# Windowed attention and soft routing on one core: values loaded straight into block-diagonal places, memory keys spread on chip, the dispatch maximum kept per token tile

## The chip, the cores and the metric

The kernel runs on one core of a Trainium2 chip. The metric is the device time of one execution in microseconds (us). The core's engines work side by side, each on its own list of instructions in order: PE (matrix products, with PEld its weight loads), DVE (vector), ACT (scalar functions), POOL (general) and SP, which here only issues DMA transfers. An engine waits at an instruction until what it needs is there; all instructions behind it wait too. SBUF is the on-chip memory of 128 partitions; PSUM takes the results of PE in eight banks.

## The reference

Three stages follow each other; 3072 tokens, 512 features.

```python
# 1. attention: 4 batches, 8 heads, head size 64, in chunks of 32 tokens
for c in range(nc):
    ...                          # keys: 16 to the left, 32 own, 8 to the right
    k_full = np.concatenate([mem_k, k_ctx], axis=2)     # and 8 memory keys in front
    v_full = np.concatenate([mem_v, v_ctx], axis=2)
    scores = scale * np.matmul(q_c, k_full.transpose(0, 1, 3, 2))
    scores = scores - np.max(scores, axis=-1, keepdims=True)
    a = np.exp(scores)
    a = a / (np.sum(a, axis=-1, keepdims=True) + 1e-09)
    out[:, :, c_start:c_end] = np.matmul(a, v_full)
# 2. soft mixture of 8 experts with 4 slots each (32 slots)
logits = x @ phi
d = softmax(logits, over tokens); slot_input = d.T @ x       # dispatch
for e in range(E):
    h = np.maximum(slot_input[e] @ w1[e], 0.0)
    slot_out[e] = h @ w2[e]
x = softmax(logits, over slots) @ slot_out                   # combine
# 3. last layer, 512 -> 1024 -> 512
h = x @ w_in
solu = h * softmax(h)
ln = (solu - mean) / np.sqrt(var + 1e-06) * g_ln
return ln @ w_out
```

## The kernel before

Attention runs in 32 groups. A group is two heads (a pair) of half the sequence of one batch: 384 tokens, 12 chunks. The two heads lie on partitions 0 to 63 and 64 to 127 of `kq`, which holds keys and queries transposed. Four groups (the four pairs of a half batch, `hb`) give three token tiles of 128 tokens with all 512 features in `xb`, and there are eight half batches.

The loop over `g` (lines 796 to 824) is software-pipelined, and its order is written by hand (`manual_schedule`): an iteration issues the QK matmuls of group g+1 (`emit_qk`), the softmax of g+1 (`emit_softmax`, whose second half normalizes the result of g-2), the loads, the PV matmuls of g-1 (`emit_pv`), the steps of the dispatch that fall due (`todo`), transposes of the outputs of g-3 (`emit_xt`) and of the exponentials of g (`emit_t`), the exp of g+1, the copy of values for g+1 (`emit_vspread`), the spread of keys for g+3 (`emit_spread`), and pieces of the conversion of w_in (`casts`).

A window of a chunk has 64 keys. The keys come in 13 records of 40 columns, 32 tokens and the 8 memory keys again in every record; `emit_spread` copies the two heads' halves into `kz`, which is block-diagonal: each head's keys have zeros on the other head's partitions, so that one matmul yields both heads. Which engine copies which half is in `SPR` ("a" ACT, "d" DVE, "p" POOL). The values likewise come as 128 rows (64 window places of each head) into `vb` and are copied by POOL into the block-diagonal `vz` (`emit_vspread`, `move`, line 294).

All large loads are issued on SP: `load_qk` (line 185, four buffers `kq`), `load_v` (line 194, four buffers `vb`), and `load_e`, which takes the next weight chunk of 512 KB from the list `chunks` (80 of them: w_in and w_out first, then the 64 of the experts in the order of use) into the next free slot; without a slot it issues none. `LOADS[g]` says how many chunks an iteration may issue. After the loop it issues as many as there are slots; later slots come free as the expert units use theirs (`release`), and the code lets SP wait for that.

The dispatch is a softmax over tokens with a running maximum: per half batch, `emit_lg` computes the logits in four partial sums on four partition blocks, ACT copies them (line 328), a matmul with `i4rep` (line 331) adds them up on every block, DVE takes the maximum over 384 tokens (line 334), ACT the exp (line 339) and a copy of the logits (line 344), three transposes and two copies (`emit_turn`, line 354) bring both to token rows, and `emit_dacc` adds to `acc`, scaled by `alpha`. Line 376 keeps the sum of the exponentials. After the last half batch `emit_slots` makes the slot inputs; then come 32 expert units (`emit_w1`, `emit_w2`), the combine softmax beside them, and the last layer, 24 token tiles.

## Time and profile before

| what | value |
|---|---|
| time, median of 3 runs | 337.04 us (336.84 to 337.57) |
| the profiled execution's own time | 337.29 us |
| its span, first to last instruction | 335.5 us |
| PE, PEld busy | 305.7 us (91%), 214.7 us (64%) |
| DVE, ACT, POOL busy | 247.1 (74%), 240.1 (72%), 192.6 us (57%) |
| HBM read, written | 80.11 MB, 16.78 MB |
| chain that ended last, by engine | PE 60%, DMA 16%, DVE 9%, ACT 8%, POOL 3% |

Busy shares are averages over stages with different limits, so they do not say what bounds the time. For that one reads the stretches of the span by themselves, which transfers are under way in them, and in the chain what each stretch waited for last. The chain is followed back from the last instruction, at each step to what released it.

### The profile page before, as it was taken

Reading aid. Unit: us, or ns where it says so; the run is one execution under the profiler, and the core shown is the slowest. Engines: PE = TensorE matmul, PEld = TensorE weight load, DVE = VectorE, ACT = ScalarE, POOL = GpSimd, SP = SyncE. Lnnn points to the kernel's source line nnn. Section 1 sums busy time; section 2 is a strip of 40 time slices with the busy share of each in tenths; the row PEclk is TensorE's granted clock in tenths of the full one; section 3 lists DMA queues with packets and bytes.
Section 4 is the critical chain, followed back from the end, with each engine's and each line's share of the span. In section 5 each row is a group of like instructions: output and inputs, shape, how many; then the busy total and the mean of one; then the engine's idle time right before and its main releaser. Section 6 shows DMA issues by size and latency. Waiting matters only on the chain.

```text
span 335.5 us, 8126 instructions
## 1 busy us (share of the span) xinstructions
PE 305.7 (91%) x2964; PEld 214.7 (64%) x2964; DVE 247.1 (74%) x445; ACT 240.1 (72%) x453; POOL 192.6 (57%) x381
## 2 busy tenths in 40 slices
PE   1998798898997989878999899999999999999995
PEld 1675565666665543322334688888888888888885
DVE  4796987988899337999207885896887989688540
ACT  3587868869886527675524879897897999788631
POOL 5587989797899113223100357776767577476600
PEclk9999999999999999999999999999999999999999
DMA  7999999999999999999950004747675675767531
GB/s 266 414 412 414 412 411 414 413 409 412 402 408 411 413 419 419 406 416 417 419 238 0 0 34 156 250 161 257 213 259 212 217 252 172 266 220 249 191 95 64
DMA packets 38920, 97.42 MB, mean 290 GB/s; under 512 B 4320, under 2 KB 14944, under 8 KB 38880
## 3 DMA queue, kind: packets, MB, share of 16 engines
q1 hardware_dynamic: 38736, 96.68, 75.2%
q8 instruction: 23, 0.38, 0.5%
q10 hardware_dynamic: 144, 0.22, 0.4%
q14 instruction: 17, 0.14, 0.1%
HBM read 80.11 MB, written 16.78 MB: 289 GB/s over the span
## 4 chain that ended last, share of the span: by engine, by line
PE 60%; DMA 16%; DVE 9%; ACT 8%; POOL 3%; issue 2%; SPq 0%; ACTq 0%; DVEq 0%; POOLq 0%
PE bank L687 36%; DMA ex_area<-in_w_dram 6%; DMA e_area<-in_w_dram 6%; DMA kq_area<-in_kr_dram 4%; PE bank L306 4%; PE h L599 4%; POOL v_area L294 2%; PE bank L246 2%; PE bank L368 2%; PE bank L317 2%; PE bank L325 1%; PE bank L461 1%; ACT s_area L278 1%; ACT s_area L320 1%; ACT kq_area L290 1%
## 5 line engine op out<-in xcount | busy, mean ns | idle before, releaser
L687 PE MATMUL bank<-wh_area,yh_area 128*128 128x512 f32 x552 | 129.6, 390 | 0.0
L687 PEld LDWEIGHTS bank<-wh_area,yh_area 128*128 128x128 f32 x552 | 103.4, 188 | 21.8
L294 POOL TENSOR_SCALAR v_area<-v_area 64x780 f32<-64x780 f32 x64 | 57.6, 900 | 14.7 <-DMA v_area<-in_vr_dram 4.8
L670 DVE STREAM_TRANSPOSE yq_area<-yq_area 128x1024 f32<-128x1024 f32 x20 | 24.9, 1245 | 23.2 <-DMA yq_area<-z 23.2
L246 PE MATMUL bank<-kq_area 128*32 128x128 f32 x768 | 29.5, 290 | 9.4 <-ACT kq_area L290 7.4
L306 PE MATMUL bank<-v_area,s_area 128*32 128x130 f32 x768 | 28.4, 280 | 8.4 <-ACT s_area L286 4.0
L677 ACT CAST yh_area<-yq_area 128x1024 fp32r<-128x1024 f32 x20 | 21.0, 1049 | 16.1 <-DVE yq_area L670 16.1
L653 POOL TENSOR_SCALAR cst_area<-cst_area 128x1 f32<-128x1 f32 x72 | 28.1, 390 | 7.1
L614 DVE SCALAR_TENSOR_TENSOR eb_area<-h,eb_area 128x1024 f32<-128x1024 f32 x24 | 28.8, 1202 | 4.6 <-ACT eb_area L608 4.3
L652 POOL TENSOR_SCALAR cst_area<-cst_area 128x1 f32<-128x1 f32 x72 | 25.8, 359 | 7.7
L246 PEld LDWEIGHTS bank<-kq_area 128*32 128x32 f32 x768 | 20.3, 114 | 15.5 <-ACT kq_area L290 9.7
L605 DVE TENSOR_REDUCE cst_area<-h 128x1 f32<-128x1024 f32 x24 | 29.0, 1216 | 0.9 <-PE h L599 0.9
L306 PEld LDWEIGHTS bank<-v_area,s_area 128*32 128x32 f32 x768 | 20.3, 110 | 14.2 <-ACT s_area L286 4.8
L608 ACT ACTIVATE eb_area<-h,cst_area 128x1024 f32<-128x1024 f32 x24 | 26.6, 1108 | 1.9 <-DVE cst_area L605 1.9
L290 ACT COPY kq_area<-kq_area 64x512 f32<-64x512 f32 x39 | 23.7, 609 | 5.8 <-DMA kq_area<-in_kr_dram 5.6
L637 ACT ACTIVATE eb_area<-eb_area,cst_area 128x1024 f32<-128x1024 f32 x24 | 27.3, 1139 | 0.1
L681 DVE TENSOR_TENSOR yh_area<-yq_area,yh_area 128x1024 fp32r<-128x1024 f32 x20 | 24.6, 1228 | 2.3 <-ACT yh_area L677 2.3
L634 ACT ACTIVATE eb_area<-eb_area,cst_area 128x1024 f32<-128x1024 f32 x20 | 23.1, 1154 | 2.4 <-DVE eb_area L614 1.4
L264 DVE TENSOR_REDUCE cst_area<-bank 128x6 f32<-128x384 f32 x32 | 17.7, 552 | 7.1 <-PE bank L246 6.6
L641 POOL TENSOR_SCALAR cst_area<-cst_area 128x1 f32<-128x1 f32 x24 | 9.0, 375 | 21.9 <-ACT eb_area L608 20.0
L320 ACT COPY s_area<-bank 128x384 f32<-128x384 f32 x32 | 15.4, 481 | 8.2 <-PE bank L317 8.0
L643 POOL TENSOR_SCALAR cst_area<-cst_area 128x1 f32<-128x1 f32 x24 | 6.4, 267 | 23.4 <-ACT eb_area L637 22.8
(150 smaller groups left out, 573.8 us busy)
## 6 DMA issues: line engine op xcount, KB each, us to landing
e_area<-in_w_dram SPq DMA_DIRECT2D x37, 512.0 KB, 8.8
kq_area<-in_kr_dram SPq DMA_DIRECT2D x32, 448.0 KB, 7.0
ex_area<-in_w_dram SPq DMA_DIRECT2D x26, 512.0 KB, 9.9
v_area<-in_vr_dram SPq DMA_DIRECT2D x32, 390.0 KB, 7.2
z<-eb_area SPq DMA_DIRECT2D x20, 512.0 KB, 3.1
yq_area<-z SPq DMA_DIRECT2D x80, 128.0 KB, 2.8
out_dram<-eb_area SPq DMA_DIRECT2D x23, 256.0 KB, 2.6
e_area<-in_w_in_dram SPq DMA_DIRECT2D x8, 512.0 KB, 8.1
```

The source lines that it names most:

```text
L246: pe.matmul(out=bk[32 * j:32 * j + 32, t * 128:(t + 1) * 128], lhsT=kq[i][:, KS + c * CH:KS + (c + 1) * CH], rhs=kwin(g % 2, c), start=Tru ...
L290: act.copy(out=o, in_=i)
L294: pool.tensor_scalar(out=o, in0=i, scalar1=1.0, scalar2=0.0, op0=ALU.mult, op1=ALU.add)
L306: pe.matmul(out=bk[32 * j:32 * j + 32, t * 2 * VW:(t + 1) * 2 * VW], lhsT=atb[g % 2][:, c * CH:(c + 1) * CH], rhs=vz[g % 2][:, :, c * VW:( ...
L605: dve.tensor_reduce(out=sc("nm", i), in_=fin["h"][i % 2], axis=AX.X, op=ALU.max, negate=True)
L608: act.activation(out=eb[i % FIN], in_=fin["h"][i % 2], func=ACTF.Exp, bias=sc("nm", i), accum_out=sc("s", i))
L614: dve.scalar_tensor_tensor(out=ub[i % FIN], in0=fin["h"][i % 2], scalar=-1.0 / FF, in1=eb[i % FIN], op0=ALU.mult, op1=ALU.mult, accum_out= ...
L637: act.activation(out=sq, in_=ub[i % FIN], func=ACTF.Square, scale=-float(FF), bias=sc("nu", i), accum_out=sc("vs", i))
L652: pool.tensor_scalar(out=t, in0=r, scalar1=r, scalar2=xx, op0=ALU.mult, op1=ALU.mult)
L653: pool.tensor_scalar(out=r, in0=t, scalar1=1.5, scalar2=r, op0=ALU.add, op1=ALU.mult)
L670: dve.transpose(out=yv[i % FIN].rearrange("p (f a t) -> p a f t", f=FC, a=4), in_=yq[i % FIN].rearrange("p (a f t) -> p a f t", f=FC, a=4),)
L687: pe.matmul(out=fin["o"][i % 2], lhsT=a[i % FIN][:, f * 128:(f + 1) * 128], rhs=w[f], start=start, stop=stop)
```

## The change

The host now lays out each half's keys as 13 x 32 tokens with the 8 memory keys in the last columns, once; `emit_spread` makes two copies per half: the tokens, into records of 40 with gaps, and the memory keys, broadcast into the gaps. The values of the two heads are loaded by two DMAs each onto the even and the odd partitions of one of four `vz`, which are zeroed once at the start; `emit_vspread` is gone. For the two heads' places to alternate, the softmax writes its differences with a stride of two. `load_v` now stands behind `emit_pv(g - 1)`, whose buffer it fills.

In the dispatch, the logits are accumulated over features in PSUM, the three token tiles on three blocks of 32 partitions; maximum, exp and sum are taken per tile and slot (96 rows), and the running maximum is kept per tile. After the last half batch the three maxima and sums are merged (`merge_max`, `merge_scale`, `merge_sum`, `merge_end`). The copies of ACT are issued at other places in an iteration (`then`, `last`). One more weight slot is there (`NE`), and `LOADS` changes.

```diff
...
-NE = 24
+NR = GT * NSLOT
+NE = 25
...
-LOADS = [0] + [1, 1, 1, 0] * 3 + [1] * 20
+LOADS = [0] + [1, 1, 1, 0] + [1] * 28
...
-SPR = ("ap", "aa", "ap", "ad")
-DUP = ("pp",)
+SPR = ("pp", "ap")
...
-KS = GREC * REC - NMEM
+KS = GREC * REC
+KT = GREC * CH
...
-    nq = KS + GTOK
+    nq = KT + GTOK
...
-    area("a1", [("v", 4 * VS), ("vz", 4 * VS)])
...
+    area("a1", [("vz", 8 * VS)])
...
-    vb = [at("v", VS * i, VS) for i in range(4)]
-    vz = [at("vz", 2 * VS * i, 2 * VS).rearrange("p (h c) -> p h c", h=2) for i in range(2)]
+    vz = [at("vz", 2 * VS * i, 2 * VS).rearrange("p (h c) -> p h c", h=2) for i in range(4)]
...
             rows = slice(64 * h, 64 * h + 64)
-            move(on, kz[g % 2][rows, KS * h:KS * h + KS], kq[g % 4][rows, 0:KS])
+            z = kz[g % 2][rows, KS * h:KS * h + KS].rearrange("p (c r) -> p c r", r=REC)
+            own = kq[g % 4][rows, 0:GREC * CH].rearrange("p (c r) -> p c r", r=CH)
+            mem = kq[g % 4][rows, KT - NMEM:KT].rearrange("p (o r) -> p o r", o=1)
+            move(on, z[:, :, 0:CH], own)
+            move(on, z[:, :, CH:REC], mem.to_broadcast([64, GREC, NMEM]))
 
     def load_v(g):
-        sp.dma_start(out=vb[g % 4], in_=vr[g])
+        for h in range(2):
+            sp.dma_start(out=vz[g % 4][h:P:2, h, :], in_=vr[g, h])
...
+            s = sb_[g % 2].rearrange("p (t k h) -> p t h k", t=GT, h=2)
...
-            mb = mx.rearrange("p (a o) -> p a o", o=1)
-            dve.tensor_tensor(out=s, in0=bk, in1=mb.to_broadcast([P, 6, WIN]), op=ALU.subtract)
+            dve.tensor_tensor(out=s, in0=bk, in1=mx.to_broadcast([P, GT, 2, WIN]), op=ALU.subtract)
...
-    def emit_vspread(g):
-        for h in range(2):
-            rows = slice(64 * h, 64 * h + 64)
-            move(DUP[g % len(DUP)][h], vz[g % 2][rows, h, :], vb[g % 4][rows, :])
...
-                    rhs=vz[g % 2][:, :, c * VW:(c + 1) * VW],
+                    rhs=vz[g % 4][:, :, c * VW:(c + 1) * VW],
...
-        act.copy(out=xtb[:, pr, :], in_=bk[:, 0:GTOK])
-
-
-    def emit_lg(hb, b=6):
+        if copy:
+            emit_xtcopy(g, b)
+
+    def emit_xtcopy(g, b=3):
+        act.copy(out=xtb[:, g % PAIRS, :], in_=bank(b)[:, 0:GTOK])
+
+    def emit_lg(hb, b=6, copy=True):
         for k in range(KC):
-            pe.matmul(
-                out=bank(b)[32 * k:32 * k + 32, 0:GTOK], lhsT=phi[:, k, :], rhs=xtb[:, k, :], start=True, stop=True
-            )
-        act.copy(out=ptb, in_=bank(b)[:, 0:GTOK])
-
-    def emit_dmax(hb, b=7):
-        pe.matmul(out=bank(b)[:, 0:GTOK], lhsT=i4rep, rhs=ptb, start=True, stop=True)
+            for t in range(GT):
+                pe.matmul(
+                    out=bank(b)[32 * t:32 * t + 32, 0:P], lhsT=phi[:, k, :], rhs=xtb[:, k, t * P:(t + 1) * P],
+                    start=(k == 0), stop=(k == KC - 1),
+                )
+        if copy:
+            emit_lgcopy(hb, b)
+
+    def emit_lgcopy(hb, b=6):
+        act.copy(out=ptb[0:NR], in_=bank(b)[0:NR, 0:P])
+
+    def emit_dmax(hb, b=6):
+        dve.tensor_reduce(
+            out=(mcol if hb else nms[0])[0:NR], in_=bank(b)[0:NR, 0:P], axis=AX.X, op=ALU.max, negate=True
+        )
         if hb:
-            dve.tensor_copy(out=alphas[hb % 2], in_=nm)
-        dve.tensor_reduce(out=mcol if hb else nm, in_=bank(b)[:, 0:GTOK], axis=AX.X, op=ALU.max, negate=True)
+            dve.tensor_tensor(out=nms[hb % 2][0:NR], in0=mcol[0:NR], in1=nms[(hb - 1) % 2][0:NR], op=ALU.min)
+
+    def emit_dexp(hb, b=6, scale=True):
+        act.activation(
+            out=dtb[0:NR], in_=bank(b)[0:NR, 0:P], func=ACTF.Exp, bias=nms[hb % 2][0:NR],
+            accum_out=(snews[hb % 2] if hb else ssum)[0:NR],
+        )
+        if scale:
+            emit_scale(hb)
+
+    def emit_scale(hb):
         if hb:
-            dve.tensor_tensor(out=nm, in0=mcol, in1=nm, op=ALU.min)
-
-    def emit_dexp(hb, b=7):
-        act.activation(out=dtb, in_=bank(b)[:, 0:GTOK], func=ACTF.Exp, bias=nm, accum_out=snews[hb % 2] if hb else ssum)
-        if hb:
-            act.activation(out=alphas[hb % 2], in_=alphas[hb % 2], func=ACTF.Exp, scale=-1.0, bias=nm)
-
-    def emit_lcopy(hb, b=7):
-        act.copy(out=dtb[0:32], in_=bank(b)[0:32, 0:GTOK])
-
-    def emit_turn(hb, rows, dst, b=6):
-        n = len(dst) * 32
-        for j in range(GT):
-            pe.transpose(
-                out=bank(b)[:, j * n:(j + 1) * n], in_=dtb[rows:rows + n, j * 128:(j + 1) * 128],
-                identity=ident[rows:rows + n, rows:rows + n],
-            )
+            act.activation(
+                out=alphas[hb % 2][0:NR], in_=nms[(hb - 1) % 2][0:NR], func=ACTF.Exp, scale=-1.0,
+                bias=nms[hb % 2][0:NR],
+            )
+
+    def emit_turned_pe(srcs, b=6):
+        for i, src in enumerate(srcs):
+            pe.transpose(out=bank(b)[:, i * NR:(i + 1) * NR], in_=src[0:NR], identity=ident[0:NR, 0:NR])
+
+    def emit_turned_act(dst, b=6):
         for i, d in enumerate(dst):
-            act.copy(
-                out=d, in_=bank(b)[:, 0:GT * n].rearrange("p (t s) -> p t s", t=GT)[:, :, 32 * i:32 * i + 32]
-            )
+            act.copy(out=d, in_=bank(b)[:, i * NR:(i + 1) * NR].rearrange("p (t s) -> p t s", t=GT))
 
     def l_of(hb):
         return L[:, hb * GT:hb * GT + GT, :]
-
-    def emit_dt(hb):
-        emit_turn(hb, 0, [l_of(hb), Db])
...
-            dve.scalar_tensor_tensor(out=ssum, in0=ssum, scalar=alpha, in1=snews[hb % 2], op0=ALU.mult, op1=ALU.add)
+            (pool if hb < HB - 1 else dve).tensor_scalar(
+                out=ssum[0:n], in0=ssum[0:n], scalar1=alpha[0:n], scalar2=snews[hb % 2][0:n],
+                op0=ALU.mult, op1=ALU.add,
+            )
             if hb == HB - 1:
-                dve.tensor_scalar(out=rcp, in0=ssum, scalar1=1e-9, scalar2=None, op0=ALU.add)
-                dve.reciprocal(out=rcp, in_=rcp)
-                dve.tensor_scalar(out=i4s, in0=i4, scalar1=rcp, scalar2=None, op0=ALU.mult)
+                merge_sum()
             dve.scalar_tensor_tensor(
                 out=acc[0:n], in0=acc[0:n], scalar=alpha[0:n], in1=bank(b)[0:n], op0=ALU.mult, op1=ALU.add
             )
...
+    def merge_max(b=6):
+
+        nm = nms[(HB - 1) % 2]
+        dve.tensor_scalar(out=nsel[0:NR], in0=sel[0:NR], scalar1=nm[0:NR], scalar2=None, op0=ALU.mult)
+        pe.matmul(out=bank(b)[0:NR, 256:256 + GT], lhsT=i4rep[0:NR, 0:NR], rhs=nsel[0:NR], start=True, stop=True)
+        dve.tensor_reduce(out=mcol[0:NR], in_=bank(b)[0:NR, 256:256 + GT], axis=AX.X, op=ALU.min)
+
+    def merge_scale():
+        act.activation(
+            out=beta[0:NR], in_=nms[(HB - 1) % 2][0:NR], func=ACTF.Exp, scale=-1.0, bias=mcol[0:NR]
+        )
+
+    def merge_sum(b=6):
+        dve.tensor_tensor(out=rcp[0:NR], in0=ssum[0:NR], in1=beta[0:NR], op=ALU.mult)
+        pe.matmul(out=bank(b)[0:NR, 320:321], lhsT=i4rep[0:NR, 0:NR], rhs=rcp[0:NR], start=True, stop=True)
+
+    def merge_end(b=6):
+        dve.tensor_scalar(out=rcp[0:NR], in0=bank(b)[0:NR, 320:321], scalar1=1e-9, scalar2=None, op0=ALU.add)
+        dve.reciprocal(out=rcp[0:NR], in_=rcp[0:NR])
+        dve.tensor_scalar(
+            out=i4s[0:NR], in0=i4[0:NR], scalar1=beta[0:NR], scalar2=rcp[0:NR], op0=ALU.mult, op1=ALU.mult
+        )
...
-                out=bank(1)[:, k * 32:(k + 1) * 32], lhsT=acc[:, k * 128:(k + 1) * 128], rhs=i4s, start=True, stop=True
+                out=bank(1)[:, k * 32:(k + 1) * 32], lhsT=acc[0:NR, k * 128:(k + 1) * 128], rhs=i4s[0:NR], start=True, stop=True
...
+        for i in range(4):
+            for h in range(2):
+                (pool if i < 3 else dve).memset(vz[i][:, h, :], 0.0)
+            if i < 2:
+                dve.memset(kz[i][0:64, KS:2 * KS], 0.0)
+                dve.memset(kz[i][64:128, 0:KS], 0.0)
         load_qk(0)
         act.dma_start(out=at("cst", 0, NCONST), in_=cst)
+        load_qk(1)
+        load_qk(2)
         load_v(0)
-        load_qk(1)
+        load_qk(3)
         load_v(1)
-        load_qk(2)
...
         emit_spread(0, "ad")
         emit_qk(0)
         emit_spread(1, "ad")
         emit_softmax(0)
         emit_exp(0)
-        emit_vspread(0)
         emit_spread(2, "ad")
-        todo = {}
+        todo, then, last = {}, {}, {}
         for hb in range(HB - 1):
-            for k, f in ((7, emit_lg), (8, emit_dmax), (9, emit_dexp), (9, emit_lcopy), (10, emit_dt), (11, emit_dacc)):
+            for k, f in (
+                (7, lambda hb: emit_lg(hb, copy=False)), (8, emit_dmax),
+                (10, lambda hb: emit_turned_pe([dtb, ptb])), (11, emit_dacc),
+            ):
                 todo.setdefault(4 * hb + k, []).append((f, hb))
+            for k, f in (
+                (7, emit_lgcopy), (9, lambda hb: emit_dexp(hb, scale=False)), 
+                (10, lambda hb: emit_turned_act([Db, l_of(hb)])),
+            ):
+                then.setdefault(4 * hb + k, []).append((f, hb))
+            last.setdefault(4 * hb + 9, []).append((emit_scale, hb))
         casts = {}
         early = {}
         for j in range(NEARLY):
             for i in range(5):
                 casts.setdefault(int(CAST0 + CASTN * j) + i, []).append((j, i))
...
-            if g + VLEAD < GROUPS:
-                load_v(g + VLEAD)
             load_e(LOADS[g])
             if 1 <= g:
                 emit_pv(g - 1)
+            if g + VLEAD < GROUPS:
+                load_v(g + VLEAD)
             for f, hb in todo.get(g, []):
                 f(hb)
+            emit_t(g)
             if 3 <= g:
-                emit_xt(g - 3)
-            emit_t(g)
+                emit_xt(g - 3, copy=False)
             emit_at(g)
+            for f, hb in then.get(g, []):
+                f(hb)
             if g + 1 < GROUPS:
                 emit_exp(g + 1)
-                emit_vspread(g + 1)
+            if 3 <= g:
+                emit_xtcopy(g - 3)
+            for f, hb in last.get(g, []):
+                f(hb)
...
-        emit_dmax(HB - 1, 0)
+        emit_dmax(HB - 1, 3)
+        merge_max()
         emit_dacc(HB - 2, steps=(1,))
         warm(TKEEP[0])
-        emit_dexp(HB - 1, 0)
-        emit_turn(HB - 1, 32, [Db], 2)
+        emit_dexp(HB - 1, 3)
+        merge_scale()
+        emit_turned_pe([dtb], 2)
+        emit_turned_act([Db], 2)
         emit_dacc(HB - 1, 5)
+        merge_end()
         warm(TKEEP[1])
         emit_slots()
-        emit_lcopy(HB - 1, 0)
-        emit_turn(HB - 1, 0, [l_of(HB - 1)], 2)
+        emit_turned_pe([ptb], 2)
+        emit_turned_act([l_of(HB - 1)], 2)
...
-    kp = kp.reshape(B, H, NREC, CH, D)
-    kp = np.concatenate([kp, np.broadcast_to(mk[:, :, None], (B, H, NREC, NMEM, D))], 3)
-    kp = np.stack([kp[:, :, i:i + GREC].reshape(B, H, GREC * REC, D)[:, :, 0:KS] for i in (0, GCH)], 1)
-    kp = kp.reshape(B, 2, PAIRS, 2, KS, D).transpose(0, 1, 2, 3, 5, 4)
-    a["kr"] = np.concatenate([kp, qv], -1).reshape(GROUPS, P, KS + GTOK)
+    kp = np.stack([np.concatenate([kp[:, :, CH * i:CH * (i + GREC) - NMEM], mk], 2) for i in (0, GCH)], 1)
+    kp = kp.reshape(B, 2, PAIRS, 2, KT, D).transpose(0, 1, 2, 3, 5, 4)
+    a["kr"] = np.concatenate([kp, qv], -1).reshape(GROUPS, P, KT + GTOK)
...
-    a["vr"] = np.ascontiguousarray(vp).reshape(GROUPS, P, VS)
+    a["vr"] = np.ascontiguousarray(vp).reshape(GROUPS, 2, WIN, VS)
...
```

## Rows read from the trace of the kernel before

**Rows 1.** The page's second part, 40 equal slices: DMA share in tenths, GB/s.

```profile
...
DMA  7999999999999999999950004747675675767531
GB/s 266 414 412 414 412 411 414 413 409 412 402 408 411 413 419 419 406 416 417 419 238 0 0 34 156 250 161 257 213 259 212 217 252 172 266 220 249 191 95 64
...
```

**Rows 2.** Stretches: length, busy us (count) of PE, PEld, DVE, ACT, POOL; clock, DMA share, GB/s.

```profile
...
80.00:97.00 17.00, 16.51 (x327) 11.77 (x330) 14.90 (x38) 15.33 (x38) 14.01 (x16) 1.00 1.02 403
...
150.00:170.00 20.00, 18.35 (x148) 7.03 (x146) 11.57 (x28) 11.43 (x28) 4.29 (x5) 1.00 1.03 417
...
172.00:174.00 2.00, 1.61 (x8) 0.32 (x8) 0.00 (x0) 0.00 (x0) 0.00 (x0) 1.00 0.36 145
...
```

**Rows 3.** DMA packets by size; issues by line with count, size, median us to landing.

```profile
...
DMA packets 38920, 97.42 MB, mean 290 GB/s; under 512 B 4320, under 2 KB 14944, under 8 KB 38880
...
e_area<-in_w_dram SPq DMA_DIRECT2D x37, 512.0 KB, 8.8
kq_area<-in_kr_dram SPq DMA_DIRECT2D x32, 448.0 KB, 7.0
ex_area<-in_w_dram SPq DMA_DIRECT2D x26, 512.0 KB, 9.9
v_area<-in_vr_dram SPq DMA_DIRECT2D x32, 390.0 KB, 7.2
...
e_area<-in_w_in_dram SPq DMA_DIRECT2D x8, 512.0 KB, 8.1
...
```

**Rows 4.** The chain that ended last, in order of time: start us, us, what.

```profile
...
117.45 0.93 PE bank L331 x2
...
124.17 1.92 PE bank L461 x16
...
133.12 9.43 DMA e_area<-in_w_dram
...
173.59 1.05 PE bank L479 x4
...
```

**Rows 5.** The SP queue's waits: total us, times, longest.

```profile
...
SPq L185 <- PE bank L246: 34.8, 25, 3.4
...
```

**Rows 6.** DMA of a stretch of the last stage, 255 to 261 us, in 40 slices; its issues.

```profile
...
GB/s 0 0 0 41 75 239 280 287 280 246 300 280 239 273 307 260 355 348 335 362 437 410 437 382 410 369 341 355 423 301 246 123 0 0 0 0 0 0 61 55
...
yq_area<-z SPq DMA_DIRECT2D x6, 128.0 KB, 2.8
...
```

**Rows 7.** Groups by line and form, first 200 us: count, busy us, mean ns; idle before.

```profile
...
L294 POOL TENSOR_SCALAR v_area<-v_area 64x780 f32<-64x780 f32 x64 | 57.6, 900 | 14.7 <-DMA v_area<-in_vr_dram 4.8 <-issue 3.7 <-PE bank L306 2.9
...
L290 ACT COPY kq_area<-kq_area 64x512 f32<-64x512 f32 x39 | 23.7, 609 | 5.8 <-DMA kq_area<-in_kr_dram 5.6
...
L269 DVE TENSOR_TENSOR s_area<-bank,cst_area 128x384 f32<-128x384 f32 x32 | 17.8, 555 | 0.7 <-ACT kq_area L290 0.4
...
L294 POOL TENSOR_SCALAR kq_area<-kq_area 64x512 f32<-64x512 f32 x15 | 9.9, 659 | 2.6 <-DVE s_area L269 1.5
...
L292 DVE COPY kq_area<-kq_area 64x512 f32<-64x512 f32 x10 | 6.2, 620 | 4.7 <-DMA kq_area<-in_kr_dram 4.5
...
L334 DVE TENSOR_REDUCE cst_area<-bank 128x1 f32<-128x384 f32 x8 | 4.4, 550 | 3.8 <-PE bank L331 3.8
...
L328 ACT COPY s_area<-bank 128x384 f32<-128x384 f32 x8 | 3.8, 476 | 9.2 <-PE bank L368 8.6 <-PE bank L325 0.6
L344 ACT COPY s_area<-bank 32x384 f32<-32x384 f32 x8 | 3.6, 456 | 0.0
...
L376 DVE SCALAR_TENSOR_TENSOR cst_area<-cst_area 128x1 f32<-128x1 f32 x7 | 2.9, 415 | 0.2 <-ACT cst_area L341 0.2
...
L354 ACT COPY cst_area<-bank 128x96 f32<-128x96 f32 x8 | 1.9, 239 | 4.4 <-PE bank L349 4.3
...
```

**Rows 8.** The SP queue in order of time, 90 to 190 us: start us, us, issues.

```profile
...
107.78 12.46 SPq L223 DMA_DIRECT2D ex_area<-in_w_dram  x13
125.26 11.29 SPq L223 DMA_DIRECT2D e_area<-in_w_dram  x13
...
```

More of the change, by code (lines that the diff above doesn't have):

```diff
@@ L154, in tile_kernel @@
     xtb = at("xt", 0, KC * GTOK).rearrange("p (k t) -> p k t", k=KC)
-    ptb = at("pt", 0, GTOK)
-    dtb = at("dt", 0, GTOK)
+    ptb = at("pt", 0, P)
+    dtb = at("dt", 0, P)
     TB = 6
@@ L171, in tile_kernel @@
     rcp = at("misc", 288, 1)
-    nm = at("misc", 290, 1)
+    nms = [at("misc", 289 + i, 1) for i in range(2)]
     mcol = at("misc", 291, 1)
@@ L175, in tile_kernel @@
     ssum = at("misc", 293, 1)
+    beta = at("misc", 297, 1)
+    sel = at("misc", 300, GT)
+    nsel = at("misc", 304, GT)
     snews = [at("misc", 294, 1), at("misc", 296, 1)]
-    cm = at("misc", 452, NTILE // 2)
-    cs = at("misc", 464, NTILE // 2)
-    small = at("misc", 480, 192)
+    cm = at("misc", 324, NTILE // 2)
+    cs = at("misc", 336, NTILE // 2)
+    small = at("misc", 352, 192)
     FIN = 2
@@ L260, in emit_softmax @@
         if g < GROUPS:
-            bk = bank(g % 2)[:, 0:GT * 128].rearrange("p (a k) -> p a k", k=WIN)
-            s = sb_[g % 2].rearrange("p (a k) -> p a k", k=WIN)
-            mx = small[:, 0:6]
-            dve.tensor_reduce(out=mx, in_=bk, axis=AX.X, op=ALU.max)
+            bk = bank(g % 2)[:, 0:GT * 128].rearrange("p (t h k) -> p t h k", t=GT, h=2)
+            s = sb_[g % 2].rearrange("p (t k h) -> p t h k", t=GT, h=2)
+            mx = small[:, 0:6].rearrange("p (t h o) -> p t h o", t=GT, o=1)
+            dve.tensor_reduce(
+                out=small[:, 0:6], in_=bk.rearrange("p t h k -> p (t h) k"), axis=AX.X, op=ALU.max
+            )
         if n >= 0:
@@ L308, in emit_pv, with emit_xt @@
                     lhsT=atb[g % 2][:, c * CH:(c + 1) * CH],
-                    rhs=vz[g % 2][:, :, c * VW:(c + 1) * VW],
+                    rhs=vz[g % 4][:, :, c * VW:(c + 1) * VW],
                     start=True, stop=True,
                 )
-    def emit_xt(g, b=3):
+    def emit_xt(g, b=3, copy=True):
         hb, pr = divmod(g, PAIRS)
@@ new lines, in emit_dmax @@
+    def emit_dmax(hb, b=6):
+        dve.tensor_reduce(
+            out=(mcol if hb else nms[0])[0:NR], in_=bank(b)[0:NR, 0:P], axis=AX.X, op=ALU.max, negate=True
+        )
+        if hb:
+            dve.tensor_tensor(out=nms[hb % 2][0:NR], in0=mcol[0:NR], in1=nms[(hb - 1) % 2][0:NR], op=ALU.min)
[6 more added lines that the diff above has]
+            emit_scale(hb)
@@ L405, in emit_c0t @@
         pe.transpose(out=bank(5)[:, 0:128], in_=at("c0", 0, P), identity=ident)
-        act.copy(out=at("misc", 300, P), in_=bank(5)[:, 0:128])
+        act.copy(out=at("c0", 0, P), in_=bank(5)[:, 0:128])
     def combine(b):
@@ L599, in emit_h @@
             pe.matmul(
-                out=fin["h"][i % 2][:, sl], lhsT=c4t(i) if i else at("misc", 300, P), rhs=m4[:, sl] if i else mps[:, sl],
+                out=fin["h"][i % 2][:, sl], lhsT=c4t(i) if i else at("c0", 0, P), rhs=m4[:, sl] if i else mps[:, sl],
                 start=True, stop=True,
@@ L762, in tile_kernel @@
     with tc.manual_schedule():
+        for i in range(4):
[4 more added lines that the diff above has]
+                dve.memset(kz[i][64:128, 0:KS], 0.0)
         load_qk(0)
         act.dma_start(out=at("cst", 0, NCONST), in_=cst)
+        load_qk(1)
+        load_qk(2)
         load_v(0)
-        load_qk(1)
+        load_qk(3)
         load_v(1)
-        load_qk(2)
         load_v(2)
-        load_qk(3)
-        for z in kz:
-            dve.memset(z[0:64, KS:2 * KS], 0.0)
-            dve.memset(z[64:128, 0:KS], 0.0)
-        for z in vz:
-            for h in range(2):
-                pool.memset(z[64 * h:64 * h + 64, 1 - h, :], 0.0)
-        dve.memset(acc, 0.0)
-        dve.memset(ssum, 0.0)
         emit_spread(0, "ad")
@@ L794, in tile_kernel @@
                 casts.setdefault(int(CAST0 + CASTN * j) + i, []).append((j, i))
+        dve.tensor_reduce(
+            out=sel, in_=ident.rearrange("p (t s) -> p t s", t=4)[:, 0:GT, :], axis=AX.X, op=ALU.add
+        )
         for g in range(GROUPS):
@@ L836, in tile_kernel @@
             emit_xt(GROUPS - 1, 1)
-        emit_dt(HB - 2)
+        emit_turned_pe([dtb, ptb])
+        emit_turned_act([Db, l_of(HB - 2)])
         if not TORD[0]:
```

10 lines of the change are left out of this document (4 added, 6 removed).

## The prediction

> **What bounds the kernel now.** I read the slices of the page first. The DMA row is at its top digit and the rate stands at 402 to 419 GB/s in every slice from the second to the twentieth, then falls: the twenty-first, which begins at 167.75 us, moves 2.0 MB, 4.8 us at the rate before it, so the stream ends at about 172.6 us [rows 1]. Stretches say the same more finely: 403 GB/s at 80 to 97 us, 417 at 150 to 170, 145 in the last two microseconds, each with PE's clock granted in full [rows 2]. Until 172.6 us the 16 DMA engines have no gap, and what they carry is a fixed list: 32 key and query loads of 448 KB, 32 value loads of 390 KB [rows 3], and the code's list of 80 weight chunks of 512 KB: 69.6 MB in all, with one small table. Read next where the chain of waits touches this list: from 133.12 us it is one weight DMA after another until 173.59, where the last expert matmuls start [rows 4]. After that no load is waited for: the 162 us left are compute that the change does not touch. The end is therefore the end of the stream plus a constant.
>
> Between 31 and 133 us the chain runs through PE, DVE, ACT and POOL, though DMA is full there too: in 80 to 97 us, of 17.0 us, PE is busy 16.5, ACT 15.3, DVE 14.9, POOL 14.0 [rows 2]. Two things are balanced there, and each could starve the other. A group with one weight chunk carries 448 + 390 + 512 KB = 1.382 MB, 3.35 us at 413 GB/s. The SP queue runs ahead of compute only as far as the four key buffers let it: its largest wait in this stage is line 185 on PE's QK matmuls, 34.8 us in 25 pieces [rows 5]. DMAs land about 7 us after their issue [rows 3]: that backlog is the cover that keeps DMA full.
>
> **The change part by part.**
> *Fewer bytes.* A row of kr shrinks from 896 to 800 columns, 384 bytes, on 32 x 128 = 4096 rows: 1.573 MB of 69.6. By bytes alone at 413 GB/s, a middling slice, that is 3.81 us. Rows also have a fixed part. With 4 KB rows alone DMA moves 417 GB/s [rows 2], so one of sixteen engines spends 157 ns on a row; the fetches of 1 KB rows in the last stage hold 239 to 307 GB/s until the next store joins them, 272 on average [rows 6], 60.2 ns. A line through both gives 0.0316 ns per byte and 28 ns fixed; 384 bytes are 12.1 ns, times 256 rows for each engine: 3.10 us. The bounds are 3.10 and 3.81; I take 3.4, since the mix with shorter rows loses only 1% against 4 KB rows (slices of 412 and 417 [rows 1]), less than a fixed 28 ns would make it lose. [...]
>
> *Value loads in two halves.* Each 390 KB load becomes two of 195 KB on 64 alternate partitions. Rows keep their 3120 bytes and their number. Every DMA brings 16 packets under 512 bytes (4320 [rows 3], for 270 DMAs by the whole view), so 32 more DMAs are 512 more, which I take as 32 per engine; between nothing and one row's fixed part each, 0 to 0.9 us; I take 0.2. The 32 more issues occupy SP about 0.35 us each, 11 us in all, hidden in its waits of 34.8 us. The rate of a 64-row load is not in the trace. The nearest rows are the fetches on 32 partitions: 272 GB/s, of whose deficit the 1 KB rows explain an unknown part [rows 6]. The cost lies between nothing (the same rows in twice as many loads) and 12.78 MB at 272 instead of 413 GB/s, 47.0 for 30.9 us, 16.1 us. I take nothing, since rows, bytes and the 16 engines stay the same and other loads are in flight beside a half load, and keep the other end for a rival. [...]
>
> *The V copy goes.* 64 copies of 900 ns on POOL [rows 7], 1.8 us per group, disappear, and the PV matmuls read what DMA wrote. In exchange load_v(g+3) waits on PE's PV of group g-1 (before, on POOL's copy, two steps earlier), and behind it on SP wait the next key load and weight chunk. PV follows QK on PE directly, so SP is released about 0.9 us later in a group than now; that comes out of the 7 us of backlog. Value data are needed four steps after the issue, so PE does not wait for them.
>
> *Memory keys on chip.* A spread of half a group was one copy of 64x512 (ACT 609 ns, POOL 659, DVE 620 [rows 7]); it becomes one of 416 columns and one of 104. The first I scale to 0.51 on ACT and 0.55 us on POOL; the second is near the 128x96 copies of 239 ns [rows 7]. ACT does 0.5 halves per group instead of 1.25: 0.76 falls to 0.38 us. DVE's 0.25 go: 0.16. POOL does 1.5 instead of 0.5 but has lost 1.8 us: 2.13 falls to 1.2.
>
> *Dispatch per token tile.* Per half batch PE loses the 128x384 matmuls of line 331 (0.93 us in the chain [rows 4]; 0.23 per group); the twelve 128-column ones instead of four of 384 are as many columns. ACT loses line 344 (456 ns) and half of line 328's 476; DVE loses over half of line 334's 550 and line 376 (415) to POOL [rows 7]: about 0.17 and 0.18 us per group. With the spreads, DVE is 0.34 and ACT 0.55 us per group lighter. Line 269 now writes with a stride of two: between nothing and its 555 ns again [rows 7]; I take nothing, because its input in PSUM is read as before; at the other end DVE is 0.2 us per group heavier than now, which feeds the second rival. Otherwise compute can follow DMA, whose group is now 400 + 390 + 512 KB, 3.23 us.
>
> *Two more chunks early, one more slot.* The new LOADS issues 30 instead of 28 chunks in the loop, so bytes that must pass during attention fall only from 42.4 to 41.8 MB: DMA is not idled by the smaller loads. The order of the 80 chunks is the same.
>
> *The merge at the end* adds nine small instructions, each at most like line 376's 415 ns [rows 7], 3.7 us, beside the last exp, transposes and dacc. The path up to 124.17 us loses the copy and matmul of lines 328 and 331 (0.48 + 0.93) and half a reduce [rows 4, 7]; I set the two against each other. Costed at nothing, since DMA sets the end; what it costs without that cover is the second rival.
>
> Sum: -3.4 + 0.2 = -3.2 us. The profiled execution took 337.29 us, its span 335.5; it becomes 334.1. The median of three runs is 337.04, 0.25 lower: **333.8 us**.
>
> **The rivals.**
> *The half loads are slower (slower than before).* For each per cent that the value stream loses, the end moves 0.31 us. The point that decides is 10%: at 370 GB/s the gain is gone. At 23% it is 30.9/0.77 - 30.9 = 9.2 us lost, 6.0 net: 343. For it: the 32-partition fetches stay near 272 GB/s [rows 6]. Against: those have 1 KB rows and nothing else in flight. Chance 0.14.
>
> *DMA runs dry at the hand-over (smaller gain).* SP issues its last free slot at 120.24 us and goes on at 125.26, after the first expert matmuls [rows 8]; DMAs landing 9.9 us after issue cover the gap, with data until about 128. After the change the slots in front of the experts hold one more chunk but 1.57 MB less has gone before: they are full 1.05 MB, 2.5 us, earlier. If the first unit stays at 124.17, DMA is idle for 1 to 2 us. It should come 1.1 us earlier, because the last keys land that much earlier (38.4 instead of 38.9 MB are issued up to them), and earlier still by the lighter engines; if these are not lighter, or SP's later release empties the backlog, 1 to 2.5 us of 3.2 are lost: 335.5. Chance 0.13.
>
> *Nothing gained:* both of these in small measure, 337. Chance 0.06.
>
> *More gain:* the dips to 402 and 408 GB/s in the eleventh and twelfth slices [rows 1] go with the lighter engines and rows cost by bytes alone: 332.6. Chance 0.13.
>
> **How the numbers follow.** Forecast 333.1 to 334.6: 0.54. A measurement can tell 0.2%, 0.7 us, from no change. Faster takes the forecast, the larger gain and the hand-over rival: 0.80; same 0.06; slower 0.14. The range leaves out the slower rival and the last of the larger gain: 332.4 to 336.9.
>
> **What would show it.** The stream should fall to nothing at about 169 us instead of 172.6, with 410 GB/s or more in each earlier slice; the first weight matmul should start before 124; from the last expert matmuls to the end should be 162 us as now. A rate below 405 in the attention stretches with SP not waiting means the half loads are slow; a gap in the DMA row near 120 to 127 means the hand-over. The prediction is wrong if the tail changes, or if the stream's end does not set it.

## The result, and the profile after

The change takes 334.43 us, the median of four runs (332.55 to 334.67), against 337.29 us of the kernel before (336.84 to 337.57) in the same session: ratio 0.9900, 95% interval 0.9884 to 0.9915, 2.9 us faster. The profiled execution took 334.36 us, its span 332.5. In a second session the same kernel took 332.94 us (332.70 to 333.58), ratio 0.9874 (0.9860 to 0.9889); between the two sessions lie 1.5 us that no edit made, and one of the four executions of the first took 332.55 us too.

The page's slices of after (against [rows 1]; a slice is 8.31 us):

```profile
DMA  7999999999999999999950004667666756666531
GB/s 286 366 359 405 407 399 411 412 411 414 409 407 396 418 417 419 415 421 416 417 228 0 0 34 158 252 206 264 207 244 211 246 209 201 240 231 234 202 95 64
```

The stream still runs without a gap and then stops: the twenty-first slice begins at 166.25 us and moves 1.9 MB, 4.6 us, so the end is at 170.8 us (before 172.6). But the second and third slices, 414 and 412 GB/s before, are 366 and 359. Stretches of after; the columns are those of [rows 2]:

```profile
10.00:20.00 10.00, 10.00 (x207) 7.91 (x207) 6.45 (x18) 5.20 (x14) 3.79 (x10) 1.00 0.97 341
20.00:40.00 20.00, 15.77 (x360) 12.84 (x361) 15.20 (x39) 12.90 (x33) 10.43 (x21) 1.00 1.02 402
...
80.00:97.00 17.00, 15.34 (x324) 11.63 (x316) 13.23 (x35) 10.94 (x31) 10.13 (x19) 1.00 1.03 410
97.00:130.00 33.00, 28.23 (x379) 16.48 (x383) 19.05 (x55) 16.76 (x50) 11.63 (x17) 1.00 1.02 411
```

At 80 to 97 us ACT's busy time fell from 15.3 to 10.9 and POOL's from 14.0 to 10.1 us, and DMA rose from 403 to 410 GB/s. The chain that ended last (start us, us, what) shows what this did; of before it ran here through PE, DVE, ACT and POOL:

```profile
11.52 1.30 PE bank L310 x24
...
20.72 0.45 SPq L202
21.22 0.59 SPq L202
21.90 6.69 DMA kq_area<-in_kr_dram
...
48.54 6.45 DMA kq_area<-in_kr_dram
55.05 6.83 DMA kq_area<-in_kr_dram
61.95 6.30 DMA kq_area<-in_kr_dram
...
122.31 1.92 PE bank L497 x16
...
161.61 9.74 DMA e_area<-in_w_dram
171.40 1.05 PE bank L515 x4
```

From 21.9 to 35.0 and from 42.9 to 94.8 us attention now waits for its key loads, one after another, and no longer for its own engines. SP's waits up to 100 us say the same (us in all, times, longest):

```profile
SPq L231 <- DMA e_area<-in_w_dram: 7.5, 9, 0.9
SPq L188 <- DMA kq_area<-in_kr_dram: 5.9, 18, 0.8
...
SPq L202 <- PE bank L310: 2.7, 1, 2.7
SPq L202 <- PE bank L254: 2.3, 7, 0.5
```

Before, SP waited 34.8 us for QK to free a key buffer [rows 5]; that wait is 0.6 us now, and SP is held mostly by transfers under way.

### The profile page after: what moved, and what is told of

It reads as the page before. It is cut to its first block, busy times and chain, and to the rows that moved or that the text cites. A ratio compares the mean times of both kernels' runs of the same rounds, so it can differ in the third digit from the quotient of the medians.

```text
span 332.5 us, 8398 instructions
## 1 busy us (share of the span) xinstructions
PE 300.8 (90%) x3069; PEld 218.1 (66%) x3069; DVE 239.4 (72%) x432; ACT 223.1 (67%) x441; POOL 169.9 (51%) x398
## 4 chain that ended last, share of the span: by engine, by line
PE 56%; DMA 32%; DVE 5%; ACT 2%; issue 2%; POOL 1%; SPq 1%; ACTq 0%; POOLq 0%
PE bank L723 37%; DMA kq_area<-in_kr_dram 19%; DMA ex_area<-in_w_dram 6%; DMA e_area<-in_w_dram 6%; PE h L635 4%; PE bank L254 3%; PE bank L310 2%; PE bank L497 1%; POOL kq_area L303 1%; PE bank L292 1%; DMA vz_area<-in_vr_dram 1%; PE bank L515 1%; PE bank L733 1%; PE t L733 1%; PE t L692 1%
## 5 line engine op out<-in xcount | busy, mean ns | idle before, releaser
L303 POOL TENSOR_SCALAR kq_area<-kq_area 64x416 f32<-64x416 f32 x88 | 38.5, 443 | 38.5 <-DMA kq_area<-in_kr_dram 27.9
L254 PEld LDWEIGHTS bank<-kq_area 128*32 128x32 f32 x768 | 21.0, 116 | 23.1 <-POOL kq_area L303 15.2
L310 PE MATMUL bank<-vz_area,s_area 128*32 128x130 f32 x768 | 29.7, 279 | 2.2 <-ACT s_area L295 1.6
L688 POOL TENSOR_SCALAR cst_area<-cst_area 128x1 f32<-128x1 f32 x72 | 26.6, 369 | 7.6
L677 POOL TENSOR_SCALAR cst_area<-cst_area 128x1 f32<-128x1 f32 x24 | 15.9, 662 | 21.7 <-ACT eb_area L644 19.8
L310 PEld LDWEIGHTS bank<-vz_area,s_area 128*32 128x32 f32 x768 | 22.3, 111 | 5.0 <-ACT s_area L295 2.8
L689 POOL TENSOR_SCALAR cst_area<-cst_area 128x1 f32<-128x1 f32 x72 | 21.9, 304 | 7.1
L741 ACT ACTIVATE eb_area<-bank,cst_area 128x512 f32<-128x512 f32 x23 | 15.8, 685 | 8.8 <-POOL cst_area L679 5.9
L299 ACT COPY kq_area<-kq_area 64x416 f32<-64x416 f32 (+1 forms) x34 | 12.2, 407 | 11.2 <-DMA kq_area<-in_kr_dram 11.1
```

Source lines behind the costliest of these rows:

```text
L254: pe.matmul(out=bk[32 * j:32 * j + 32, t * 128:(t + 1) * 128], lhsT=kq[i][:, KT + c * CH:KT + (c + 1) * CH], rhs=kwin(g % 2, c), start=Tru ...
L303: pool.tensor_scalar(out=o, in0=i, scalar1=1.0, scalar2=0.0, op0=ALU.mult, op1=ALU.add)
L310: pe.matmul(out=bk[32 * j:32 * j + 32, t * 2 * VW:(t + 1) * 2 * VW], lhsT=atb[g % 2][:, c * CH:(c + 1) * CH], rhs=vz[g % 4][:, :, c * VW:( ...
L688: pool.tensor_scalar(out=t, in0=r, scalar1=r, scalar2=xx, op0=ALU.mult, op1=ALU.mult)
```

## The experiments

*The loads by themselves.* A kernel with nothing but loads on SP, in eight stages of 24: chunks of 4096-byte rows, keys of 3584, keys of 3200, values whole, as halves on alternate partitions, as halves on 64 neighbouring partitions, and two mixes of key, chunk and value (whole; alternate halves). It leaves out all of the computation. The two kinds of halves differ in one line:

```python
sp.dma_start(out=b[h:P:2, 0:780], in_=vr[i, h])
...
sp.dma_start(out=b[64 * h:64 * h + 64, 0:780], in_=vr[i, h])
```

> This kernel leaves out all of the computation; it only loads, in eight stages with a pause between: 24 loads each of 4096-byte rows, 3584-byte rows, 3200-byte rows, value rows of 3120 bytes as one load of 128 partitions, the same as two halves on alternate partitions, the same as two halves on contiguous partitions, then the mix of a group (3200, 4096, 3120) with whole values, then the mix with alternate halves. Theory A (the half loads cost nothing by themselves, the loss is a hole at the start): stage 5 runs within 3% of stage 4, and the last mix within 1% of the one before it. Theory B (half loads are slow by themselves): stage 5 is more than 8% below stage 4, and the last mix 2 to 3% below the one before. Rows: if a row has a fixed part of 13 to 28 ns, 3584-byte rows run at 410 to 414 GB/s and 3200-byte rows at 405 to 411; by bytes alone all stages of 128 partitions run at about 417. [...]

One stretch within each stage, in this order (length, DVE and POOL busy, clock, DMA share, GB/s):

```profile
8.00:26.00 18.00, 4.93 (x6) 0.00 (x0) 1.00 1.01 400
46.00:64.00 18.00, 0.00 (x0) 0.00 (x0) 1.00 1.02 408
82.00:96.00 14.00, 0.00 (x0) 0.00 (x0) 1.00 1.03 415
114.00:126.00 12.00, 0.00 (x0) 0.00 (x0) 1.00 1.03 412
146.00:170.00 24.00, 0.00 (x0) 0.00 (x0) 1.00 0.95 306
186.00:214.00 28.00, 0.00 (x0) 0.00 (x0) 1.00 1.04 240
231.00:245.00 14.00, 0.00 (x0) 0.00 (x0) 1.00 1.03 416
264.00:281.00 17.00, 0.00 (x0) 0.00 (x0) 1.00 1.03 414
```

Rows of 3200 bytes run at 415 GB/s, those of 3584 at 408; the rates show no fixed part of a row. The trace's records of single rows do: 126 ns for 3200 bytes, 140 for 3584, 159 for 4096 (medians, the same for such rows in before and in after). A straight line through the first two leaves some 9 ns that do not grow with the bytes. Alternate halves reach only 306 GB/s by themselves, yet cost nothing in the mix (414 against 416). Neighbouring halves are slow themselves: 240 GB/s with the DMA engines fully busy (1.04). SP's list shows what held the alternate ones (start us, us, what; x is the count issued without a break):

```profile
108.47 19.39 SPq L47 DMA_DIRECT2D buf<-in_vr_dram  x24
...
139.68 30.58 SPq L52 DMA_DIRECT2D buf<-in_vr_dram  x48
```

SP took 0.64 us for each half of 195 KB, without a wait for any transfer, and 199,680 bytes in 0.64 us are 312 GB/s. A row of 3120 bytes takes 124 ns there (median) as in whole loads, and 220 in neighbouring halves. So the alternate halves alone were held by their issue, as far as these records show; what stretched the 6% of their rows that took over 250 ns, which the share of 0.95 counts in, is open. In the mix a set of three loads takes 3.25 us and its four issues 1.78, so the issue hides behind larger loads. Of the two theories expected neither holds whole: the halves are slow by themselves, and the mix loses nothing.

*Neighbouring halves in the kernel.* After, with

```diff
-            sp.dma_start(out=vz[g % 4][h:P:2, h, :], in_=vr[g, h])
+            sp.dma_start(out=vz[g % 4][64 * h:64 * h + 64, h, :], in_=vr[g, h])
```

and the softmax without its stride.

> The changed kernel with each head's values loaded onto 64 contiguous partitions instead of alternate ones, and the softmax written without the stride of two. [...] Without the stride the softmax writes may be faster, which moves nothing as long as DMA sets the pace.

Its shortest execution took 378.91 us, with a mean granted clock of 0.96; three others took 386.97 to 388.30 with 0.94 to 0.95, and the page is of one of these. Even the shortest is 44 us above the change. The slices of the page:

```profile
DMA  8999999999999999999999900036766666666631
GB/s 253 282 285 271 253 263 261 266 263 267 269 272 260 260 253 243 364 418 420 415 421 418 394 33 0 29 136 231 249 223 219 228 217 228 221 225 224 229 131 55
```

Where values are part of the stream it runs at 243 to 285 GB/s, and at 415 to 421 once only weight chunks are left: one slow load of three slows the mix to two thirds. That the places alternate is what makes the V part possible. Why loads onto neighbouring partitions are slower (240 GB/s by themselves) is not shown.

*The parts alone.* Before, with the keys part alone (rows of 800 columns, two copies for each half, all else as it was):

```diff
-    nq = KS + GTOK
+    nq = KT + GTOK
...
-            move(on, kz[g % 2][rows, KS * h:KS * h + KS], kq[g % 4][rows, 0:KS])
...
+            move(on, z[:, :, 0:CH], own)
+            move(on, z[:, :, CH:REC], mem.to_broadcast([64, GREC, NMEM]))
```

> The kernel before with the memory keys spread on chip and nothing else of the change: 1.573 MB less to load, two copies per half instead of one, V copy, dispatch, LOADS and slots as before. Theory 1 (bytes alone decide, and 3200-byte rows cost by their bytes, as the loads alone showed): 3.8 us less, 333.5. Theory 2 (compute and DMA were balanced, so without lighter engines the attention runs no faster and DMA goes thin in it): 335 to 337.5, with DMA below 405 GB/s between 30 and 100 us and a later start of the expert units.

It is slower: 339.57 us (337.54 to 340.15), ratio 1.0058 (1.0038 to 1.0078), with 1.57 MB less to load, and slower than either theory had it. Two of its stretches, and SP's largest wait in attention:

```profile
60.00:80.00 20.00, 17.86 (x361) 12.79 (x353) 18.31 (x48) 16.34 (x46) 17.47 (x21) 1.00 0.98 364
80.00:97.00 17.00, 15.46 (x269) 11.10 (x269) 14.18 (x35) 14.27 (x42) 13.09 (x17) 0.90 0.99 367
```

```profile
SPq L186 <- PE bank L251: 37.9, 23, 4.1
```

ACT's two copies per half, by tile shape (x count | busy us, mean ns | idle before):

```profile
L295 ACT COPY kq_area<-kq_area 64x416 f32<-64x416 f32 x39 | 20.6, 529 | 4.8 <-DMA kq_area<-in_kr_dram 4.5
L295 ACT COPY kq_area<-kq_area 64x104 f32<-64x104 f32 x39 | 10.7, 273 | 0.0
```

They take 802 ns for the 609 of one copy before [rows 7]. ACT, DVE and POOL stand at 16.3, 18.3 and 17.5 of 20 us, and SP waits for QK 37.9 us. Fewer bytes were bought with time on engines that had none. The granted clock fell to 0.90 in the second stretch, but executions whose mean clock was 0.998 or 0.999 took 338.82 to 340.15 us too, so the loss is not the clock's.

The V part alone (halves, no copy, `load_v` behind PV, start order and `SPR` of the change; keys, `LOADS` and dispatch as before):

```diff
-        sp.dma_start(out=vb[g % 4], in_=vr[g])
+        for h in range(2):
+            sp.dma_start(out=vz[g % 4][h:P:2, h, :], in_=vr[g, h])
...
-                emit_vspread(g + 1)
```

> The kernel before with the V part of the change alone: values loaded by halves into block-diagonal places, no copy on POOL, load_v behind PV, the loads of the start and the division of the spreads as in the change; key rows of 896 columns, dispatch, LOADS and slots as before. Theory 1 (DMA full before and after, so only bytes move the end): no gain, 337 to 338.5, the upper end with the thin stretch at the start. Theory 2 (the lighter POOL is itself worth something): 336 or less.

337.63 us (336.80 to 338.74), ratio 1.0006 (0.9994 to 1.0019): nothing. DMA is full (408 GB/s at 20 to 40 and at 60 to 80 us, 390 between) and has as many bytes to carry as before; POOL's 17.0 us of 20 fell to 10.5 (40 to 60 us) for nothing.

Both together, with the `LOADS` of the change, and dispatch and `NE` of before:

> Both the keys and the V part with the change's LOADS, on the dispatch and the 24 slots of before. If removing the V copy is what lets attention follow DMA with the smaller loads, nearly the whole gain: 333 to 334.5, though the keys alone gave 339.6 and the V part alone should give 337 to 338.5. If the lighter dispatch is needed as well, 335 to 337.

334.38 us (333.11 to 335.48), ratio 0.9907 (0.9888 to 0.9927): the ratio of the whole change in the first session; in the second the change was 1.1 us lower (0.9874), with intervals that just overlap. The edits do not add up: +2.1 and +0.1 us alone, -3.1 us together. `LOADS` changed with them; both parts with the `LOADS` of before were not run, so its share of the 3.1 is open.

*The V copy put back.* After, with values loaded whole into `vb` and copied by POOL as before (`load_v` ahead of `load_e`, `SPR` of before, no stride), so keys, dispatch and `LOADS` remain:

> The changed kernel with the V path of before: one load of 128 partitions into vb, POOL's copies into two vz, no stride in the softmax, load_v ahead of the weight chunk and not behind PV, and the spreads divided over the engines as before. If the V part of the change gives nothing by itself and costs only the thin stretch at the start, this is faster than the changed kernel by 1 to 2 us: 332.5 to 333.3. If the copies on POOL hold attention up, DMA goes thin later and the time is 334.5 or more.

336.94 us (335.21 to 339.25), ratio 0.9990 (0.9965 to 1.0014): by the median the gain is gone. POOL is busy 16.6 to 17.9 of 20 us between 20 and 80 us, DMA falls to 388 GB/s at 97 to 130 and 381 at 130 to 150 us, and 8% of the chain is POOL's V copy.

```profile
97.00:130.00 33.00, 26.62 (x344) 16.77 (x346) 16.10 (x47) 14.62 (x44) 16.32 (x18) 0.90 0.98 388
```

Part of this is PE's clock (third number from the right): it was granted at 0.90 here and at 1.00 in after. Six executions with a mean granted clock of 0.99 took 337.64 to 339.25 us, the profiled one among them; the six with 0.993 to 1.00 took 335.21 to 336.24, which leaves 1.2 to 2.2 us of the gain. Why the clock fell is open. Against the keys alone it is 2.6 us faster: where the engines are the bound, the rest of the change (dispatch, `LOADS`, the order at the start) does count; which of these was not taken apart.

*The bytes put back.* The kernel with keys and V part, and 96 columns in each row of `kr` that nobody reads:

```diff
-    nq = KT + GTOK
+    nq = KT + GTOK + 96
...
+    a["kr"] = np.concatenate([kp, qv, np.zeros(qv.shape[:-1] + (96,), f)], -1).reshape(GROUPS, P, KT + GTOK + 96)
```

> The kernel with the keys and the V part of the change (334.38 us) and, in every row of kr, 96 more columns that nobody reads: 3584 bytes as before for 3200, 1.573 MB more in all; instructions and their order are the same. If the gain is the bytes that the stream no longer carries, they come back at the attention's rate: 1.573 MB at 411 GB/s, 3.8 us, 338.2 us (337.5 by the prediction's 3.1 us), as slow as the kernel with the V part alone, which carries the same bytes (337.63). If a good part of the gain came from lighter work on the engines, the time stays near 334.4 to 336, with the rate in the attention stretches below 405 GB/s.

336.85 us (335.82 to 338.37), ratio 0.9982 (0.9967 to 0.9998). The instructions are the same, so the bytes are worth 2.5 us (336.85 - 334.38; by the two intervals 1.7 to 3.4): most of the 3.1, and less than the 3.8 expected; the 336.85 us lie between the two theories. With these bytes the last expert matmuls start at 174.67 us, as with the V part alone; without them at 170.18, in an execution that was the shortest of its six.

*Work put on POOL in the copy's place.* After, with seven copies of 128x32 on POOL per iteration:

```diff
+                for _ in range(7):
+                    pool.tensor_scalar(
+                        out=at("spare", 0, 32), in0=ident[:, 0:32], scalar1=1.0, scalar2=0.0, op0=ALU.mult, op1=ALU.add
+                    )
```

> The changed kernel with seven copies of 128x32 on POOL in each iteration, from a constant into a place that nobody reads, where the V copy stood: about 1.6 to 1.9 us of POOL time per group that nothing waits for but POOL's own next instruction. If POOL's time was what held the variant with V copies at 336.9, this gives 335.5 to 337.5 too, with DMA thin somewhere between 60 and 150 us. If it was the copies' place in the chain from load to PV, this stays at 333 to 334.4.

363.86 us (362.27 to 364.69), ratio 1.0773: far beyond what was expected. A stretch of its attention, and POOL's two groups from 20 to 150 us (line, engine, operation, tiles | busy us, mean ns | idle before):

```profile
40.00:60.00 20.00, 12.80 (x265) 10.19 (x267) 9.98 (x28) 10.20 (x30) 16.77 (x50) 0.97 0.83 284
```

```profile
L866 POOL TENSOR_SCALAR s_area<-cst_area 128x32 f32<-128x32 f32 x189 | 45.8, 242 | 14.1
L303 POOL TENSOR_SCALAR kq_area<-kq_area 64x416 f32<-64x416 f32 x78 | 33.8, 439 | 3.5
```

The error was mine in the expectation: with `SPR` of the change POOL does 1.5 halves of the keys per group and the w_in sums, some 2.1 us per group (47.9 us between 20 and 97 us, at 3.4 us a group); (242 + 75) ns x 7 is 2.2 more. That is 4.3 us for a group of 3.4; 0.9 x 32 groups is 29 us, near the 29.4 measured. By this sum POOL became the bound, and from 40 to 56 us the chain runs through POOL. The change leaves it about 1.3 us per group free, of the 1.8 that the V copy took: the spreads could go to POOL only because the copy went. Whether the V copy's time or its place in the chain from load to PV held v_copy, this run does not tell.

*The hole at the start.* SP's list of after from 9 to 15 us:

```profile
9.63 0.43 SPq L234 DMA_DIRECT2D e_area<-in_w_in_dram  x1
12.88 1.12 SPq L202 DMA_DIRECT2D vz_area<-in_vr_dram  x2
14.11 0.51 SPq L188 DMA_DIRECT2D kq_area<-in_kr_dram  x1
```

`load_v(4)` waits for PV of group 0, which ends at 12.82 us in the chain, and the next key load stands behind it. What was issued until 10.06 us lasts until about 14.4; then the rate falls, as DMA in 40 slices of 0.4 us from 8 to 24 us shows:

```profile
GB/s 391 414 421 406 383 431 424 394 406 392 319 376 428 442 410 398 213 304 289 213 271 352 324 342 321 349 312 261 262 287 312 358 375 457 351 427 349 422 422 404
```

To take the wait off SP, `load_v(g + 2)` was put ahead of `load_e`, where its buffer has long been free:

```diff
+            if g != 1 and g + 2 + (g == 0) < GROUPS:
+                load_v(g + 2 + (g == 0))
             load_e(LOADS[g])
...
-            if g + VLEAD < GROUPS:
-                load_v(g + VLEAD)
```

> The changed kernel, with the value load of group g+2 instead of g+3 issued in an iteration, ahead of the weight chunk, so that SP never waits for a PV that is not long done. Theory A: the wait of SP on the PV of group 0 at 12.9 us and the thin stretch of DMA from 14 to 22 us (0.85 MB less than before between 8 and 24 us, 2 us) go, and the time falls by 1.5 to 2 us against the changed kernel, to about 332.6. Theory B: the rate between 14 and 22 us stays near 300 GB/s and the time stays within 0.5 us of 334.4.

In the profile the hole is gone (407 GB/s at 10 to 20 us for 341) and the last expert matmuls start at 169.57 us for 171.40. In time: 333.23 us (332.80 to 333.64), ratio 0.9874 (0.9861 to 0.9887), 1.2 us below the first session's 334.43 and 0.3 above the second's 332.94. So the same kernel was measured once more:

> The changed kernel as it is, beside the others on the same chip. All theories: 0.988 to 0.992 of the kernel before, about 334.2; DMA thin again between 14 and 22 us, since it comes from the order of issues and not from chance.

It was faster than expected, and its profile has a smaller hole (381 GB/s at 10 to 20 us), though no issue was moved; its last expert matmuls start at 170.06. What differs first is PE. PV of group 0 took 1.30 us in the first profile (the first line of the chain shown above) and 0.67 here (chain of after_again; 21 of its 24 matmuls recorded), and SP went on at 12.21 us for 12.88:

```profile
11.48 0.67 PE bank L310 x21
```

The granted clock reads 1.00 in both, so why PE was slower is open. In the V part alone `load_v` waits for PV too, SP goes on at 11.60 us, and there is no hole:

```profile
10.00:20.00 10.00, 9.23 (x219) 7.14 (x222) 7.09 (x18) 5.58 (x12) 3.10 (x5) 1.00 1.03 408
```

So the order of issues opens the way for a hole; how large it gets depends on when PV of group 0 ends and on the bytes issued until then. Up to 20 us the first profile of after moved 6.47 MB, this one 6.86, late_v 7.11, before 7.04. Bytes and stream end go together in these profiles, but the medians do not separate late_v from after.

Chunks brought forward to fill the hole, `LOADS = [1, 2, 1, 1, 0] + [1, 1, 1, 0] * 2 + [1] * 20`:

> The changed kernel with two weight chunks more in the first two iterations (1 and 2 instead of 0 and 1) and two less later (none in iterations 8 and 12), in all 30 as before. Theory A: 1.05 MB, 2.5 us of work, lie in the queues while SP waits for the PV of group 0, so the stretch from 14 to 22 us stays above 390 GB/s; 332.5 to 333. Theory B: 334.4, with the low rate wherever value halves are in flight.

333.97 us (332.91 to 335.24), ratio 0.9899 (0.9881 to 0.9917), not the 332.5 to 333 expected. The start is full (413 GB/s), but in the iterations that now load no chunk it drops to 391 (40 to 60 us): the hole moved, nothing won. Last, late_v with a chunk in every iteration, `LOADS = [1] * 33`:

> late_v with a weight chunk in every iteration (32 instead of 30 in the loop). It lays one chunk more in the queues at the start and one in iteration 4. If what is left between late_v's 402 to 412 GB/s in attention and the 414 of the loads alone is a queue that is not deep enough, 0.5 to 1 us less than late_v: 332.3 to 332.8. If it is not, 333.2 as late_v; slower only if attention ends so much later that the slots fill before the first expert unit.

332.68 us (332.60 to 332.96), ratio 0.9865 (0.9853 to 0.9878), the fastest kernel measured here. Its interval overlaps that of after in the same session, so that it beats the change is not shown.

## Why the prediction was right, and where its steps were not

*The bound.* Right: the end is the end of the stream plus a constant. The last expert matmuls moved from 173.59 [rows 4] to 171.40 us, and from them to the end of the span it is 161.1 us, 161.9 before. The 0.8 us lie behind the last output store: from its issue to the end 3.4 us in the one profile of before, 2.6 in those of after and late_v; why stays open. It is 2.6 to 2.8 in eleven of the twelve other profiles, with the keys or the V part alone too, and 3.1 in pool_load's, so the 3.4 is more likely that one execution's than the change's. The stream ended at 170.8 us, not at about 169, after slices of 359 to 407 GB/s where 410 or more was forecast.

*Fewer bytes.* Taken at 3.4 us, with bounds of 3.10 and 3.81. A row's 140 ns fell to 126; 14 ns on 256 rows of each engine are 3.6 us, so the size was near. The fixed 28 ns per row, drawn from fetches of 1 KB rows [rows 6], are some 9 for these rows. What the kernel gets of it is 2.5 us (fat_rows), since its stream does not hold its rate everywhere. Of the 3200-byte rows 99%, loaded by themselves, took the same 126 ns.

*Value loads in two halves.* Right at nothing, and the rival is refuted: 414 GB/s for 416 in the mix. The row that the other end rested on [rows 6] was no measure of it; a half load alone is held at 306 GB/s by SP's issue, as far as the records show. An issue of a half was taken at 0.35 us; in the kernel two took 1.11 to 1.12 us where nothing held them.

*SP's release.* This step failed. "That comes out of the 7 us of backlog" is right from about 21 us to the end of attention, where no wait of SP for PE is longer than 0.6 us. It is not at the start, where the first PV ends only at 12.82 us: SP stood idle 2.7 us there, and between 8 and 24 us 5.76 MB passed, for 6.61 before, 0.85 MB or 2.1 us. By the profiles that is about what is missing between the 3.6 us of bytes and the 1.8 us by which the stream ended earlier. In the second profile, with the faster PV, 6.17 MB passed, and 1.1 us are lost. I had read the backlog where it is deepest, not where the loop begins.

*Copies and spreads.* The sizes were near: a spread's token copy took 538 ns on ACT and 554 on POOL (taken 0.51 and 0.55 us), the memory keys' 275 and 331 (taken 239). "Compute can follow DMA" was one sentence for the step that decided. It held, but without the V copy's end it would not have: keys alone lose 2.1 us, and the V copy put back takes all of the gain or, where the clock held, half of it. A chance of its own should have stood there; that the engines might not get lighter is only a clause of the hand-over rival, and that the spreads of the keys by themselves cost more than their bytes save is nowhere.

*Dispatch, and the stride of two.* Costed at nothing, and they brought little: keys and V alone are at 0.9907 of before, the whole change at 0.9900 and 0.9874, so between nothing and 1.1 us (with the 25th slot). The merge did not hold up the experts: their first unit starts 1.9 us earlier than before. The subtraction with the stride took 560 ns, 555 without it [rows 7].

*The hand-over.* No gap: the first expert unit starts at 122.31 us for 124.17 [rows 4], and DMA moves 411 GB/s at 97 to 130 us.

*The sum.* 3.2 us forecast, 2.9 measured in the first session and 4.5 in the second. It met the first in part because errors cancelled, which is luck: the hole at the start (about 2 us) was not seen, and neither was the end shorter by 0.8 us. The second lies near where the rival *more gain* was put (332.6).
